# K and V chunks as one transfer over 128 partitions instead of two over alternate partitions

## The chip, the cores and the metric

The kernel runs on one core of a Trainium2 chip. The metric is the device time of one execution in microseconds (us), lower is better. The kernel before took 215.94 us (median of 3 runs, 215.93 to 216.82). A run counts as slow when it is over 1.5% above the fastest run of the same kernel; all comparisons below use fast runs, unless a sentence says otherwise.

Some terms. HBM is the large memory where the inputs lie, SBUF the memory on the chip with 128 rows, called partitions. PE (TensorE) does the matrix products, VectorE (DVE) and ScalarE (ACT) the rest, and the sync queue (SP) issues transfers. A transfer is one issued load; the 16 DMA engines carry it out in packets, and each engine ends its part with a 4-byte semaphore packet that reports it done. A transfer has landed when all 16 have reported. The cadence is the time from the landing of one chunk to the landing of the next.

## The reference, cut to what matters

One decoding step: an attention block over a long cache, beside a small mixer and MLP block, added together.

```python
# x [4, 1, 576]; k_cache, v_cache [B=4, Hkv=16, Sk=8192, Dh=128], bf16; 32 query heads
W = min(4096, max(256, Sk // 4))                   # 2048: only the last 2048 tokens count
k = jnp.repeat(k_cache[:, :, Sk - W:, :], 2, axis=1)
v = jnp.repeat(v_cache[:, :, Sk - W:, :], 2, axis=1)
p = softmax(einsum("bhqd,bhkd->bhqk", q, k) * Dh ** -0.5)
o = einsum("bhqk,bhkd->bhqd", p, v) ... @ wo
# + B block: layernorm, w1 [576, 576], w2, w3 [576, 4608], w4 [4608, 576]
```

The windows of K and V have 4 x 16 x 2048 x 128 bf16 elements each, 33.6 MB. Both together are 67.1 MB of the 88.5 MB that the kernel has to read. Each byte is loaded once.

## The kernel before

K and V come in 16 chunks each. A chunk is one batch and four heads (2 MB); it fills one of the four slots of a ring in SBUF. Partition 4i + g of a slot holds 64 tokens in a row of head g: 16384 bytes that are contiguous in HBM and in SBUF. All loads but the small x are issued from one queue, the sync queue. A slot is refilled when PE has transposed (K) or multiplied (V) what was in it.

```python
NPOS = 4                                    # slots of the ring
ring_t = sb("ring", [128, NPOS * UE], BF16) # UE = 64 tokens x 128 = 8192 elements
...
def kv_pairs(cache, c):                     # the two halves of a chunk
    b, gq = CH[c]
    dst = lambda a: ring_t[a:128:2, (c % NPOS) * UE:(c % NPOS + 1) * UE]
    src = cache[b, NU * gq:NU * gq + NU, Sk - W:Sk, :].rearrange("g (i t) d -> i g (t d)", t=NT)
    return [(dst(a), src[:, a:NU:2, :]) for a in range(2)]
for c in range(NC):
    add_dma(kv_pairs(A_k_cache, c), ("k", c % NPOS), [t_done(c - NPOS)] if c >= NPOS else [], c)
for c in range(NC):
    add_dma(kv_pairs(A_v_cache, c), ("v", c % NPOS), [f"PV{c - NPOS}" if c >= NPOS else t_done(c + NC - NPOS)], KS + c)
...
# PE: before the first transpose of a K chunk, and before the products of a V chunk
w = [take(("k", c % NPOS), 32)] if k == 0 else []     # 16 for each of the two halves
...
# every such wait is emitted in one helper (line 584 of the kernel)
engine.wait_ge(S[w[1]], w[2]).then_inc(S[w[1]], -w[2])
```

A half has 64 partitions, every second one. PE waits for both halves of a chunk, so the halves are never used one by one.

## Time and profile before

| | before |
|---|---|
| time, median of 3 | 215.94 us |
| span in the profile | 214.1 us |
| moved by DMA | 88.66 MB, 7459 packets |
| K and V issues | 64 of 1024 KB |
| 16384-byte data packets | 4096 for K and V, median 613 ns |

The last row is from the packet records of the trace. The next lines are from the page of the kernel before: the span; the busy share of the 16 DMA engines in 40 slices (9 is nine tenths or more) and the GB/s of each slice; the packets; the sync queue's own row (packets, MB, share of the engines' time); the lines of the chain that ended last; and the K and V issues with the KB of each and the median us from issue to landing.

```profile
span 214.1 us, 5906 instructions
...
DMA  7999999999999999999999999999999999999992
GB/s 282 404 385 445 441 407 438 419 427 416 435 429 429 422 435 429 424 426 435 429 426 426 429 429 425 419 432 429 429 422 429 435 429 419 430 436 426 428 409 104
DMA packets 7459, 88.66 MB, mean 414 GB/s; under 512 B 1292, under 2 KB 1688, under 8 KB 2456
...
q1 hardware_dynamic: 7432, 88.50, 97.7%
...
DMA w<-in_B_w_dram 15%; SPq L177 1%; PE ps L421 1%; PE ps L438 1%; DVE out_sb L560 0%
...
ring<-in_A_k_cache_dram SPq DMA_DIRECT2D x32, 1024.0 KB, 13.0
ring<-in_A_v_cache_dram SPq DMA_DIRECT2D x32, 1024.0 KB, 15.1
```

The DMA engines are at nine tenths or more in every slice but the first and the last. A K half lands 13.0 us after its issue although it takes 2.4 us to move: the rest is waiting behind other transfers in the queue.

The stretch table of the kernel before gives, for each stretch, busy us of each engine with the number of instructions, then the granted clock, the DMA share (packet time over the time of 16 engines; it can pass 1 because the records of neighbouring packets overlap by a few ns) and GB/s:

```profile
core 0: us, PE busy (x) PEld busy (x) DVE busy (x) ACT busy (x) POOL busy (x), PEclk, DMA share, GB/s
...
34.00:100.00 66.00, 64.26 (x1060) 51.74 (x1052) 42.06 (x66) 39.84 (x43) 3.81 (x13) 1.00 1.01 427
100.00:130.00 30.00, 21.69 (x389) 16.53 (x388) 17.42 (x29) 16.34 (x23) 0.00 (x0) 0.82 1.01 428
130.00:180.00 50.00, 19.63 (x674) 18.97 (x674) 4.69 (x14) 0.00 (x0) 0.00 (x0) 0.50 1.01 427
```

From 34 to 180 us the DMA share is 1.01, whatever PE does: PE is busy 64.26 of 66 us in the K stage and 19.63 of 50 us in the V stage, and the rate is 427 or 428 GB/s in both. The Trainium skill ("DMA: Bandwidth & Descriptors", Specifications) gives 435 GB/s as the ceiling on the SBUF side; the trace agrees to 2%.

The sync queue's own waits (us in total, times, longest) show that the queue that issues the transfers has nothing to do most of the time:

```profile
SPq L177 <- PE ps L340: 84.8, 16, 27.9
SPq L177 <- PE ps L421: 46.1, 12, 11.0
SPq L177 <- DVE out_sb L560: 31.8, 1, 31.8
```

And one line from PE's waits:

```profile
engine line waited for: us in total, times, longest us
PE ps L421 <- PEq L584: 37.7, 13, 3.2
```

The wait is put down to PE's sequencer at line 584. That is the helper line of the kernel that takes a semaphore.

The end of the chain in order of time (start, us, what):

```profile
179.19 31.22 DMA w<-in_B_w_dram
...
210.46 1.39 PE ps L438 x18
211.85 0.44 DVE out_sb L560
```

A w4 load that was issued at 179.2 us lands at 210.4 us, and PE, VectorE and the store follow.

### The profile page before, as it was taken

To read this page: it belongs to the slowest core of one execution; us is meant where nothing else is said; L and a number is where in the kernel's file an instruction comes from. 1 tells how busy PE (TensorE), PEld (TensorE's weight loads), DVE (VectorE), ACT (ScalarE), POOL (GpSimd) and SP (SyncE) were. 2 spreads that over 40 slices of the span, in tenths; PEclk is the share of its full clock that TensorE was granted. 3 is DMA by queue.
4 is the path that set the end of the run, shared out by engine and by line. 5 is a ranking of instruction groups with operands and counts; after the bars stand their busy time and mean duration, and the time that the engine had idled before them with its cause. 6 is when DMAs were issued, how large, how long until landed. Compare 5 with 4: busy or idle time off the path is not lost. (4 is left out here: it accounts for less than half of the span.)

```text
span 214.1 us, 5906 instructions
## 1 busy us (share of the span) xinstructions
PE 145.6 (68%) x2642; PEld 108.9 (51%) x2646; DVE 76.5 (36%) x150; ACT 61.0 (29%) x75; POOL 10.9 (5%) x37
## 2 busy tenths in 40 slices
PE   0157787999999999999996178033444333336995
PEld 0023312888878887888774068033434333334542
DVE  5305400577676676666664830100010011001000
ACT  2001402466655665666666620000000000000000
POOL 8301000000001000000000000000000000000000
PEclk9999699999999999999999655555555555555799
DMA  7999999999999999999999999999999999999992
GB/s 282 404 385 445 441 407 438 419 427 416 435 429 429 422 435 429 424 426 435 429 426 426 429 429 425 419 432 429 429 422 429 435 429 419 430 436 426 428 409 104
DMA packets 7459, 88.66 MB, mean 414 GB/s; under 512 B 1292, under 2 KB 1688, under 8 KB 2456
## 3 DMA queue, kind: packets, MB, share of 16 engines
q1 hardware_dynamic: 7432, 88.50, 97.7%
q8 instruction: 8, 0.13, 0.2%
q14 instruction: 3, 0.02, 0.0%
q10 hardware_dynamic: 16, 0.01, 0.0%
HBM read 88.49 MB, written 0.00 MB: 413 GB/s over the span
## 5 line engine op out<-in xcount | busy, mean ns | idle before, releaser
L340 PE MATMUL ps<-perm_bf,ring 128*128 128x128 bf16 x1024 | 61.7, 220 | 0.6
L340 PEld LDWEIGHTS ps<-perm_bf,ring 128*128 128x128 bf16 x1024 | 57.5, 98 | 8.9 <-issue 8.6
L347 DVE COPY kt<-ps 128x1024 bf16<-128x1024 bf16 x80 | 52.3, 687 | 24.8 <-PE ps L340 24.3
L421 PE MATMUL ps<-PTpad,ring 128*128 128x8 bf16 x1024 | 29.7, 168 | 41.2 <-PEq L584 37.7
L346 ACT ACTIVATE kt<-ps 128x1024 bf16<-128x1024 bf16 x48 | 48.5, 1023 | 29.1 <-PE ps L340 28.3
L421 PEld LDWEIGHTS ps<-PTpad,ring 128*128 128x128 bf16 x1024 | 28.7, 104 | 42.3 <-issue 42.2
L561 ACT ACTIVATE out_sb<-ps 4x288 bf16<-4x288 f32 x1 | 0.4, 401 | 87.2 <-PE ps L438 87.2
L354 PE MATMUL ps<-kt,Qs 128*32 128x512 bf16 x272 | 17.8, 382 | 1.4 <-PEq L584 1.4
L410 DVE TENSOR_TENSOR PTpad<-PT,mU_bf 128x512 bf16<-128x512 bf16 x16 | 6.4, 420 | 29.7 <-PE ps L421 29.7
L433 DVE TENSOR_TENSOR OTn<-ps,rinvB 128x32 bf16<-128x32 f32 x4 | 0.8, 191 | 34.2 <-PE ps L421 34.2
L523 PE MATMUL ps<-w,x1nT 128*32 128x384 bf16 (+2 forms) x65 | 11.3, 766 | 0.8 <-DMA w<-in_B_w_dram 0.5
L354 PEld LDWEIGHTS ps<-kt,Qs 128*32 128x32 bf16 x272 | 5.8, 96 | 6.8 <-issue 1.5
L375 POOL COPY Qs<-Qpad 128x128 bf16<-128x128 bf16 x16 | 4.6, 293 | 87.0 <-PE ps L354 75.0
L301 PE MATMUL ps<-kt,xnT 128*32 128x512 bf16 x32 | 3.6, 631 | 4.3 <-DMA kt<-in_A_wq_dram 4.3
L523 PEld LDWEIGHTS ps<-w,x1nT 128*32 128x32 bf16 x65 | 3.3, 113 | 6.3 <-issue 3.9
L438 PE MATMUL ps<-w,ORT 128*4 128x288 bf16 x64 | 5.8, 357 | 0.4 <-DVE ORT L460 0.4
L278 PE MATMUL ps<-ident_bf,xn_bf 4*128 4x4 bf16 x8 | 0.6, 170 | 8.0 <-DVE ragsrc L271 8.0
L560 DVE CAST out_sb<-ps 4x288 bf16<-4x288 f32 x1 | 0.4, 446 | 14.5 <-PE ps L438 14.5
L438 PE MATMUL ps<-w,h2T_sb 128*4 128x288 bf16 x72 | 5.0, 286 | 0.4 <-DMA w<-in_B_w_dram 0.4
L392 PE MATMUL ps<-kt,permT_bf 128*128 128x512 bf16 x3 | 1.8, 608 | 4.9 <-DVE kt L391 4.8
L544 DVE COPY h2T_sb<-ps 128x16 bf16<-128x16 bf16 x1 | 0.2, 166 | 13.6 <-PE ps L538 13.6
L438 PEld LDWEIGHTS ps<-w,ORT 128*4 128x4 bf16 x64 | 3.3, 106 | 3.1 <-DVE ORT L460 1.0
(99 smaller groups left out, 61.6 us busy)
## 6 DMA issues: line engine op xcount, KB each, us to landing
ring<-in_A_k_cache_dram SPq DMA_DIRECT2D x32, 1024.0 KB, 13.0
ring<-in_A_v_cache_dram SPq DMA_DIRECT2D x32, 1024.0 KB, 15.1
w<-in_B_w_dram SPq DMA_DIRECT2D x2, 2304.0 KB, 22.9
w<-in_A_wo_dram SPq DMA_DIRECT2D x2, 2304.0 KB, 20.3
kt<-in_A_wq_dram SPq DMA_DIRECT2D x1, 4096.0 KB, 12.2
w<-in_B_w_dram SPq DMA_DIRECT2D x1, 2592.0 KB, 27.4
w<-in_B_w_dram SPq DMA_DIRECT2D x3, 576.0 KB, 14.5
w<-in_B_w_dram SPq DMA_DIRECT2D x1, 1296.0 KB, 30.0
```

Source lines behind the costliest of these rows:

```text
L301: ins = e.matmul(Qps[k][32 * g:32 * g + 32, :], lhsT=x_, rhs=w, start=(r == 0), stop=(r == 4), tile_position=(0, 32 * g), skip_group_check ...
L340: ins = e.transpose(tb[n % 4][:, t, :], slot_t(c)[:, 8 * k + t, :], perm_bf[:])
L346: return "act", lambda e: e.activation(out=ktbuf[:, n % 16], in_=tb[n % 4], func=ACTF.Copy)
L347: return "dve", lambda e: e.tensor_copy(out=ktbuf[:, n % 16], in_=tb[n % 4])
L354: ins = e.matmul(Sps[32 * u:32 * u + 32, q, :].rearrange("p (t i) -> p t i", t=16), lhsT=Qs[:, c % NPOS, 32 * u:32 * u + 32], rhs=ktgrp[:, ...
L375: P(lambda e, c=c, cc=cc: e.tensor_copy(out=Qs[:, c % NPOS, :], in_=Qpad_t[:, 128 * cc:128 * cc + 128]), waits=["qT", "qs_zero"] + ([f"SC{ ...
L392: add("pe", lambda e, q=q: e.matmul(ps[:, 4 + q % 3, :], lhsT=permT_bf[:], rhs=PTx[:, q, :], start=True, stop=True), waits=[f"PTx{q}", "pe ...
L410: return lambda e: e.tensor_tensor(out=PTpad[:, c % 2], in0=PTv[:, :, cc, :].unsqueeze(2).to_broadcast([128, NT, NU, 2]), in1=mU_bf[:].uns ...
L421: ins = e.matmul(o_, lhsT=slot_t(c)[:, t, :], rhs=PTpad[:, c % 2, t].rearrange("p u e -> p (u e)"), start=(t == 0), stop=(t == NT - 1))
L433: add("dve", lambda e, hv=hv: e.tensor_tensor(out=hv(OTn), in0=OTps.rearrange("p (b h) -> p b h", b=B), in1=hv(rinvB), op=ALU.mult), waits ...
L438: return e.matmul(ACC[h], lhsT=lhsT, rhs=rhs, start=start, stop=stop, tile_position=(0, 32 * h), skip_group_check=True)
L523: ins = e.matmul(H2ps[k][32 * g:32 * g + 32, 128 * off:128 * (off + cnt)].rearrange("p (c x) -> p c x", c=cnt), lhsT=x_, rhs=w.rearrange(" ...
```

## The change

The intent: half as many transfers for K and V, each twice as large, all partitions at once; fewer issues and fewer completions for the same bytes.

```diff
         def kv_pairs(cache, c):
             b, gq = CH[c]
-            dst = lambda a: ring_t[a:128:2, (c % NPOS) * UE:(c % NPOS + 1) * UE]
-            src = cache[b, NU * gq:NU * gq + NU, Sk - W:Sk, :].rearrange("g (i t) d -> i g (t d)", t=NT)
-            return [(dst(a), src[:, a:NU:2, :]) for a in range(2)]
+            return [(ring_t[:, (c % NPOS) * UE:(c % NPOS + 1) * UE],
+                     cache[b, NU * gq:NU * gq + NU, Sk - W:Sk, :].rearrange("g (i t) d -> i g (t d)", t=NT))]
...
-                w = [take(("k", c % NPOS), 32)] if k == 0 else []
+                w = [take(("k", c % NPOS), 16)] if k == 0 else []
...
-            ... take(("v", c % NPOS), 32) ...
+            ... take(("v", c % NPOS), 16) ...
```

More of the change, by code (lines that the diff above doesn't have):

```diff
@@ L428, in bass_parallel_sum__sliding_block_cached__mixer_s_mlp__decode_kernel @@
             add("dve", dve_pad(c), waits=w, inc=[(tok("pad"), 1)], key=KV + 2 * max(c - 1, 0) + 0.2)
-            add("pe", pe_PV(c), waits=[take("pad"), take(("v", c % NPOS), 32)] + ([take("otn")] if b == 0 else []), sig=f"PV{c}",
+            add("pe", pe_PV(c), waits=[take("pad"), take(("v", c % NPOS), 16)] + ([take("otn")] if b == 0 else []), sig=f"PV{c}",
                 key=KV + 2 * c, loop=("V", gq))
```

## The prediction

> **What bounds the kernel now.** The DMA engines, all the time. The page of the kernel before moves 88.66 MB in a span of 214.1 us, DMA at nine tenths in all slices but the first and last. The stretch table has a DMA share of 1.01 at 427 to 428 GB/s from 34 to 180 us. The chain of waits ends in a w4 load that was issued at 179.2 us and landed at 210.4, plus 18 matmuls, one copy and the store. No wait of PE for a K or V load is in the list of waits. The Trainium skill ("DMA: Bandwidth & Descriptors", Specifications) gives a ceiling of 435 GB/s at the SBUF side; this trace is within 2% of it in these stretches.
>
> **What the change does.** It removes 32 of 64 transfers of 1024 KB: 32 issues on the sync queue (median 600 ns for K, 572 ns for V) and, per DMA engine, 32 semaphore packets of 4 bytes (9 ns each in the trace's packet records). It adds nothing. The data packets stay 4096 of 16384 bytes, median 613 ns; only their order changes (four heads in turn instead of two and two). The compute engines' order is the same. PE waited for both halves before, so the grain of compute, the ring and the issue waits stay. The same skill page (Rules for kernel authors) says that two transfers to disjoint partition sets serialize on the same 16 engines and one transfer should be used. It doesn't say how large the gain is in a full queue.
>
> **How much is on the critical path.** Sync queue: none. A K chunk takes 4.89 us to move (from the landings), issuing its halves took about 1.2 us, and a half lands a median 13.0 us (K) or 15.1 us (V) after issue, so its fixed costs hide behind queued transfers. Semaphore packets: at most 32 x 9 ns = 0.29 us per engine. Comparing cadences suggests less: the halves land every 2.446 us, that is 611.6 ns per packet with its quarter of a semaphore; the second wo load (eight packets of 18432 bytes per engine, one semaphore) took 5.50 us and the first w4 load (eight of 20736) 6.18 us. From these three I estimate 0.0368 ns per byte, some 10 ns per packet, and about zero for a transfer. So the gain is between 0 and 0.3 us of 215.9.
>
> **Prediction.** 215.7 us, 8 in 10 between 215.0 and 216.7 (the three runs before spread from 215.93 to 216.82). Chances: faster by over 2% 0.01, within 2% 0.95, slower by over 2% 0.04.
>
> **What would show it.** K and V as 32 transfers of 2048 KB with the DMA share still 1.01 and 426 to 430 GB/s in the same stretches; a K chunk landing every 4.88 to 4.90 us; 16384-byte packets still at 613 ns; about 512 fewer small packets; the chain still ending in the same w4 load at about 210 us.
>
> **What would make it wrong.** Another order of reads (each engine now steps through four heads 2 MB apart) that slows packets above 613 ns: 3% would cost 5 us. Two engines meeting at one port. A longer stall at the first K issue (5.6 us now, from 5.3) that runs the queue dry. A different placing of the instruction fetches, which already leave some engines 1.9 us behind others at the end (landing records of the last w4 load): about 1 us either way.

## The result, and the profile after

| | before | after |
|---|---|---|
| median us (6 runs each) | 216.02 (215.91 to 217.14) | 216.04 (215.88 to 216.50) |
| ratio of the fast runs | | 0.9991, 95% interval 0.9966 to 1.0015 |
| K and V issues | 64 of 1024 KB | 32 of 2048 KB |

Ratios here and below are the mean time of one kernel's fast runs over that of the kernel before in the same rounds, so they are not quite the ratio of the medians in the text. The time is the same. The lines of the page of the changed kernel that answer to those above:

```profile
span 214.7 us, 5874 instructions
...
DMA  7999999999999999999999999999999999999992
GB/s 276 409 381 443 436 413 433 437 424 411 412 424 430 433 433 424 427 429 433 421 430 424 427 436 419 427 427 430 424 427 424 430 430 427 427 432 432 417 413 78
DMA packets 6946, 88.65 MB, mean 413 GB/s; under 512 B 780, under 2 KB 1176, under 8 KB 1944
...
q1 hardware_dynamic: 6920, 88.50, 97.4%
...
DMA w<-in_B_w_dram 15%; SPq L177 1%; PE ps L420 1%; PE ps L437 0%; DVE out_sb L559 0%
...
ring<-in_A_k_cache_dram SPq DMA_DIRECT2D x16, 2048.0 KB, 11.5
ring<-in_A_v_cache_dram SPq DMA_DIRECT2D x16, 2048.0 KB, 16.6
```

The same bytes, 513 packets fewer (the counts under 512 B fell from 1292 to 780, which is 32 semaphore packets on each of 16 engines), and the same share and rate in the slices. A K chunk lands 11.5 us after its issue (a half 13.0), a V chunk 16.6 us (a half 15.1).

The stretch table of the changed kernel, same columns:

```profile
34.00:100.00 66.00, 64.64 (x1038) 52.03 (x1029) 41.10 (x64) 38.31 (x42) 3.52 (x12) 0.97 1.01 427
100.00:130.00 30.00, 22.61 (x402) 17.58 (x396) 18.41 (x31) 17.06 (x24) 0.29 (x1) 0.85 1.01 428
130.00:180.00 50.00, 20.16 (x695) 19.45 (x692) 4.70 (x14) 0.00 (x0) 0.00 (x0) 0.50 1.01 427
```

The DMA share and the rate did not move: 1.01 at 427, 428 and 427 GB/s.

The sync queue's waits after the change:

```profile
SPq L177 <- PE ps L339: 100.9, 16, 32.7
SPq L177 <- PE ps L420: 52.7, 12, 11.7
SPq L177 <- DVE out_sb L559: 33.1, 1, 33.1
```

The three totals were 84.8 + 46.1 + 31.8 = 162.7 us and are now 100.9 + 52.7 + 33.1 = 186.7 us, 24.0 us more. Issuing K and V took 41.8 us before and takes 23.2 us now; the 18.6 us that the queue saved went into waits: it is done issuing sooner and then waits longer for PE to empty a slot.

The end of the chain after the change:

```profile
178.91 32.92 DMA w<-in_B_w_dram
...
211.88 0.58 PE ps L437 x6
212.46 0.43 DVE out_sb L559
```

It still ends in a w4 load, but in the next of the five, 1.4 us later; that load landed at 211.11 us before, so it is 0.7 us later here. (In the second trace of the changed kernel, below, the chain ends in the same load as before, at 210.8 us.) This profiled run was the slowest of the six (216.5 us), with a span 0.6 us longer. The landing records show where that comes from. The 16 engines finish the last w4 load between 209.58 and 212.06 us here, and between 209.54 and 211.47 us before: the first engine is done at the same time, and the last one lags by 2.47 us instead of 1.93 us.

The landing records also give the cadence: when the last engine's share of K chunk 0 and of K chunk 15 landed, and the difference divided by 15. It is worked out from the traces for all the kernels that leave the queue open:

```
kernel              chunk 0    chunk 15   us per chunk   data packet, median / mean ns
before              36.35      109.74     4.893          16384 B: 613 / 614.9
after               36.31      109.88     4.904          16384 B: 613 / 615.9
after_again         36.31      109.79     4.898          16384 B: 614 / 615.6
four_by_head        36.39      109.81     4.894          16384 B: 611 / 614.3
two_by_column       36.23      110.99     4.984           8192 B: 313 / 314.0
eight_by_column     36.61      112.14     5.035           8192 B: 309 / 318.0
contiguous_halves   42.41      185.28     9.525          16384 B: 1206 / 1189.3
```

A chunk in one transfer takes as long as a chunk in two, to within 0.011 us.

### The profile page after: what moved, and what is told of

Read it like the earlier page. It is cut to its first block, busy times and chain, and to the rows that moved or that the text cites. A ratio compares the mean times of both kernels' runs of the same rounds, so it can differ in the third digit from the quotient of the medians.

```text
span 214.7 us, 5874 instructions
## 1 busy us (share of the span) xinstructions
PE 147.2 (69%) x2642; PEld 111.2 (52%) x2646; DVE 76.2 (35%) x150; ACT 60.2 (28%) x75; POOL 10.9 (5%) x37
## 2 busy tenths in 40 slices
DMA packets 6946, 88.65 MB, mean 413 GB/s; under 512 B 780, under 2 KB 1176, under 8 KB 1944
## 5 line engine op out<-in xcount | busy, mean ns | idle before, releaser
L339 PEld LDWEIGHTS ps<-perm_bf,ring 128*128 128x128 bf16 x1024 | 58.8, 99 | 7.1 <-issue 6.8
L345 ACT ACTIVATE kt<-ps 128x1024 bf16<-128x1024 bf16 x48 | 47.7, 1023 | 29.3 <-PE ps L339 29.3
L522 PE MATMUL ps<-w,x1nT 128*32 128x384 bf16 (+1 forms) x65 | 11.1, 766 | 0.4 <-DVE x1nT L497 0.4
L437 PE MATMUL ps<-w,ORT 128*4 128x288 bf16 x64 | 5.0, 324 | 0.4 <-DVE ORT L459 0.4
L437 PEld LDWEIGHTS ps<-w,h2T_sb 128*4 128x4 bf16 x72 | 2.8, 84 | 4.0 <-DMA w<-in_B_w_dram 3.0
## 6 DMA issues: line engine op xcount, KB each, us to landing
ring<-in_A_k_cache_dram SPq DMA_DIRECT2D x16, 2048.0 KB, 11.5
ring<-in_A_v_cache_dram SPq DMA_DIRECT2D x16, 2048.0 KB, 16.6
```

The costliest lines, as they stand in the source:

```text
L339: ins = e.transpose(tb[n % 4][:, t, :], slot_t(c)[:, 8 * k + t, :], perm_bf[:])
L345: return "act", lambda e: e.activation(out=ktbuf[:, n % 16], in_=tb[n % 4], func=ACTF.Copy)
L437: return e.matmul(ACC[h], lhsT=lhsT, rhs=rhs, start=start, stop=stop, tile_position=(0, 32 * h), skip_group_check=True)
L522: ins = e.matmul(H2ps[k][32 * g:32 * g + 32, 128 * off:128 * (off + cnt)].rearrange("p (c x) -> p c x", c=cnt), lhsT=x_, rhs=w.rearrange(" ...
```

## The experiments

Theory A: the DMA engines are the bound, and a transfer has next to no cost of its own while others are queued behind it. Rival B: a transfer does cost something, and the changed order of reads lost as much as the merging gained. Rival C: PE, busy 97% of the K stage, is the real bound, so nothing done to DMA can show. Where no base is named, the edits are to the kernel before.

### The changed kernel again, and four transfers per chunk

The first is the changed kernel as it is, with five rounds.

> The changed kernel once more, for a narrower interval. Theory A (the DMA engines are the bound, and a transfer in a full queue costs next to nothing by itself): ratio to the kernel before 0.998 to 1.001, that is 0 to 0.3 us. Rival B (each transfer removed gains its fixed cost, but the new order of reads loses as much): the same ratio, so this run alone does not tell them apart; B needs 16384-byte packets slower than 613 ns, which the trace of the first run does not show.

Measured: 216.10 us against 216.14 us, ratio 0.9989 (0.9968 to 1.0010). The same again.

The second has one transfer per head, 512 KB each, so 64 transfers more than before:

```diff
-            dst = lambda a: ring_t[a:128:2, ...]
+            dst = lambda a: ring_t[a:128:4, ...]
-            return [(dst(a), src[:, a:NU:2, :]) for a in range(2)]
+            return [(dst(a), src[:, a:a + 1, :]) for a in range(NU)]
-                w = [take(("k", c % NPOS), 32)] ...      # and the same for V
+                w = [take(("k", c % NPOS), 64)] ...
```

> Each chunk as four transfers of 512 KB, one head each: 64 transfers more than the kernel before, same packets of 16384 bytes, another order of reads. Theory A: between 0 and +0.6 us (64 times at most one 9 ns semaphore packet), chunk still every 4.89 us, packets at 613 ns. Rival B (a transfer has a real cost in the queue, which the changed kernel's read order hid): clearly slower, for 0.1 us per transfer +6 us.

Measured: 216.06 us, ratio 0.9990 (0.9969 to 1.0010). Lines of its page:

```profile
DMA packets 8483, 88.66 MB, mean 413 GB/s; under 512 B 2316, under 2 KB 2712, under 8 KB 3480
...
ring<-in_A_k_cache_dram SPq DMA_DIRECT2D x64, 512.0 KB, 8.6
ring<-in_A_v_cache_dram SPq DMA_DIRECT2D x64, 512.0 KB, 13.3
```

One, two and four transfers per chunk, with three different orders of reads, take 216.1, 216.1 and 216.1 us; the cadence is 4.898, 4.893 and 4.894 us. For rival B to hold at any size that matters, the order of reads would have to cancel the cost at all three counts, and the packets would have to be slower by as much. Their means are 615.6, 614.9 and 614.3 ns: 1.3 ns between the ends, times 256 packets per engine, is 0.3 us. A trade of that size between packets and transfers can't be excluded, since the times don't resolve it. Theory A stands. The interval leaves room for the predicted gain of 0 to 0.3 us (0.14%), but not for 0.1 us per transfer.

### Smaller packets, same number of transfers

Two transfers over all 128 partitions, each with half the columns:

```diff
-            dst = lambda a: ring_t[a:128:2, (c % NPOS) * UE:(c % NPOS + 1) * UE]
+            HU = UE // 2
+            dst = lambda a: ring_t[:, (c % NPOS) * UE + a * HU:(c % NPOS) * UE + (a + 1) * HU]
-            return [(dst(a), src[:, a:NU:2, :]) for a in range(2)]
+            return [(dst(a), src[:, :, a * HU:(a + 1) * HU]) for a in range(2)]
```

> Two transfers of 1 MB per chunk as before, but over all 128 partitions and half the columns each, so 8192-byte packets, twice as many. From the estimate of 10 ns per packet (256 more per DMA engine) theory A expects +2.4 us, ratio about 1.011, the chunk every 5.04 us. If only the number of transfers or of partitions mattered, it would be +0.0.

Measured: 218.30 us, ratio 1.0093 (1.0073 to 1.0112), 2.16 us more than the median before. Lines of its page and of its stretch table:

```profile
DMA packets 11555, 88.66 MB, mean 410 GB/s; under 512 B 1292, under 2 KB 1688, under 8 KB 2456
...
q1 hardware_dynamic: 11528, 88.50, 98.2%
```

```profile
34.00:100.00 66.00, 63.38 (x1040) 50.71 (x1035) 41.38 (x64) 39.17 (x43) 3.81 (x13) 1.00 1.01 421
```

So the split that keeps the number of transfers costs 2.16 us, and the split that doubles it at the same packet size (four_by_head) costs nothing. The packets count, not the transfers. The 4096 additional packets are 256 per engine: 2.16 us / 256 = 8.4 ns each in the time; the cadence of K says (4.984 - 4.893) us / 8 = 11.4 ns. That cadence is a mean which two long gaps (5.05 and 5.08 us) raise; by the medians of the gaps, 4.974 and 4.893 us, it is 10.1 ns. The estimate was 10. Whether the cost is the packet's own or comes from the shorter run that is read from HBM, this run does not separate. The cadence of 5.04 us in the expectation was an error of arithmetic: 4.893 us plus 8 x 10 ns is 4.97 us.

### Eight transfers per chunk

Head by head and half the columns, 256 KB each, with the packets of the experiment above:

```diff
+            HU = UE // 2
+            dst = lambda g, a: ring_t[g:128:4, (c % NPOS) * UE + a * HU:(c % NPOS) * UE + (a + 1) * HU]
+            return [(dst(g, a), src[:, g:g + 1, a * HU:(a + 1) * HU]) for a in range(2) for g in range(NU)]
```

> Eight transfers of 256 KB per chunk (one head, half the columns), 8192-byte packets as in the two-by-column kernel, 192 transfers more than it. Theory A: within 0 to +1.7 us of the two-by-column kernel as long as the sync queue can issue eight in 4.9 us (8 times 0.53 to 0.60 us is 4.3 to 4.8, just enough). Rival B: far slower; if issue becomes the limit the DMA share drops below 1 and the sync queue shows no waits.

Measured: 220.87 us median, but scattered from 218.54 to 222.45 us. Two of the six runs count as slow, the profiled one too; they look like the upper end of the scatter, for a fast run had as low a clock (0.788 against 0.790 and 0.791). The four fast ones give a ratio of 1.0162 (1.0120 to 1.0205), 1.5 us more than the two-by-column kernel (1.0162 - 1.0093 of 216 us). The chain of its profiled run and a line of its stretch table:

```profile
SPq L177 14%; DMA w<-in_B_w_dram 10%; PE ps L422 1%; PE ps L439 1%; DVE out_sb L561 0%
```

```profile
34.00:100.00 66.00, 64.62 (x1035) 52.04 (x1032) 41.08 (x64) 38.21 (x42) 3.52 (x12) 0.97 1.01 409
```

Now the sync queue is 14% of the chain: issuing eight transfers at a median of 594 ns takes 4.75 us of a cadence of about 5 us, and its waits fall to 42.0 us in all (154.9 in the two-by-column kernel). So the issue comes close to being the limit. That it is one, this run does not show: the DMA share stays at 1.01 in the line above (at 409 GB/s in place of 421), and the expectation named a share below 1 and no waits as the signs. Because of the scatter it gives no clean cost per transfer either. It agrees with the range expected (0 to 1.7 us), no more.

### Where the fixed cost is: one transfer in flight

The queue waits for every K and V transfer to land before it issues the next. It is done once with the changed kernel (32 transfers of 2 MB) and once with the kernel before (64 of 1 MB). As the waiting takes the semaphore, the queue itself tells PE afterwards:

```diff
+        def add_alone(pairs, skey, waits, key):
+            def emit(e):
+                for o_, i_ in pairs:
+                    e.dma_start(o_, i_).then_inc(S["lone"], 16)
+                    e.wait_ge(S["lone"], 16).then_inc(S["lone"], -16)
+                e.sem_inc(S[skey], 16)        # 32 in the kernel with two halves
+            add("sp", emit, waits, None, key)
-            add_dma(kv_pairs(A_k_cache, c), ...)   # and the same for V
+            add_alone(kv_pairs(A_k_cache, c), ...)
```

> The changed kernel, but the sync queue waits for each K and V transfer to land before it issues the next: one transfer of 2 MB in flight. This exposes a transfer's fixed cost. [...] Theory A expects 32 transfers with about 2 us each exposed: +55 to +75 us over 216, each 6.5 to 7.2 us from issue to landing.

> The kernel before, with the same wait after each of its 64 transfers of 1 MB. Theory A expects twice the fixed cost of the one-transfer form: a difference between the two of 32 times about 2 us, +50 to +75 us, so about 330 to 350 us in all. Rival (merging never matters, whatever the queue holds): the two forms equal.

Measured: 305.82 us in the first, 376.84 us in the second (the kernel before on the same chip: 216.59 us). The DMA row and the K and V issues, of the first and then of the second:

```profile
DMA  8999567665766777766676668576666766678994
...
ring<-in_A_k_cache_dram SPq DMA_DIRECT2D x16, 2048.0 KB, 7.3
ring<-in_A_v_cache_dram SPq DMA_DIRECT2D x16, 2048.0 KB, 7.4
```

```profile
DMA  8996555555555555545655547555555555555795
...
ring<-in_A_k_cache_dram SPq DMA_DIRECT2D x32, 1024.0 KB, 4.8
ring<-in_A_v_cache_dram SPq DMA_DIRECT2D x32, 1024.0 KB, 4.8
```

The DMA engines now stand idle between transfers. The kernel with half the transfers is 71.0 us faster, 71.0 / 32 = 2.22 us for each transfer less. Against the open queue the exposed cost is (305.82 - 216.59) / 32 = 2.79 us per transfer of 2 MB and (376.84 - 216.59) / 64 = 2.50 us per transfer of 1 MB. The 2 us of both expectations is the fixed cost that the Trainium skill ("DMA: Bandwidth & Descriptors", Anatomy of one DMA) gives for transfers on the gpsimd path (about 2.0 us). These transfers go by the sync queue, and they show somewhat more; the issue (a median of 534 to 535 ns in both traces) is a part of it. So both totals were expected too low: the first at +55 to +75 us, measured +89, with 7.3 us to landing in place of 6.5 to 7.2; the second at 330 to 350 us, measured 376.84. The difference between the two, 71.0 us, is inside the +50 to +75 expected, and the rival (no difference) falls. So the cost that the change removes is real, and it is large where it is exposed. In the kernel as it is, it is not exposed.

### How full the queue has to be

The kernel before with at most two transfers of 1 MB in flight: before each issue the queue waits for the transfer before the last one.

```diff
+                for n, (o_, i_) in enumerate(pairs):
+                    if len(flight) == 2:      # 3 in the third kernel
+                        land(e)               # wait for the oldest; tell PE if its chunk is whole
+                    k = count[0] % 2
+                    count[0] += 1
+                    e.dma_start(o_, i_).then_inc(S[("pair", k)], 16)
+                    flight.append((k, skey if n == 1 else None))   # 2 MB transfers: skey always
```

> The kernel before, with at most two transfers of 1 MB in flight: the sync queue waits for the transfer before the last one to land before each issue. Theory A: a fixed cost of about 2 us fits under the other transfer's 2.45 us, so nearly all of it vanishes: 216 to 225 us, DMA share 0.95 or more in the middle.

Measured: 229.64 us, ratio 1.0609 (1.0558 to 1.0659), more than the 216 to 225 us expected; the DMA share from 34 to 100 us was 0.93, below the 0.95 expected:

```profile
34.00:100.00 66.00, 59.88 (x934) 48.09 (x932) 37.48 (x58) 35.83 (x39) 3.26 (x11) 0.95 0.93 371
```

Two runs were made to see what two in flight lack: a third transfer of 1 MB, and two of 2 MB with the changed kernel.

> At most three transfers of 1 MB in flight, where two gave 229.6 us (13 us more than an open queue, more than expected). Theory D: what two in flight lost is not only the fixed cost but the engines' lag behind each other (1.5 to 2 us after an instruction fetch), which one transfer of slack cannot cover; a third transfer (2.45 us more) covers both: 216 to 219 us. Rival E (the waits themselves cost the sync queue time at every transfer): still 225 us or more.

> The changed kernel with at most two transfers of 2 MB in flight. Theory D: the slack is one whole transfer of 4.9 us, which covers the fixed cost of about 2.4 us and a lag of 2 us: 216 to 219 us, so that with a shallow queue the larger transfer does gain, some 11 us against two transfers of 1 MB in flight. Rival E, a cost for every wait: half of the 13 us, 222 us.

Measured: 219.78 us for three of 1 MB (218.94 and 220.62; ratio 1.0177, 1.0084 to 1.0269), a little over the 216 to 219 us expected. A line of the stretch table of its profiled run, a fast one:

```profile
150.00:190.00 40.00, 14.30 (x499) 13.93 (x500) 2.99 (x9) 0.00 (x0) 0.00 (x0) 0.50 0.98 401
```

For two of 2 MB, 221.94 us in a fast run and 226.89 us in a slow one. That was repeated with five rounds:

> The same kernel as the one with two transfers of 2 MB in flight, because one of its two runs was in the slow state (226.9 us) and the other fast (221.9 us). If theory D's slack of a whole transfer were enough, its fast runs would be at 216 to 219 us; the one fast run says about 222 us. The trace should show where the loss sits: in idle DMA engines (DMA share below 1) or in longer packets (mean of the 16384-byte packets above 615 ns at a DMA share of 1).

Measured: 218.79, 219.31 and 220.31 us in the three fast runs, 222.37 to 223.02 us in the three slow ones; ratio 1.0155 (1.0131 to 1.0179). A line of the stretch table of its profiled run, which is a slow one:

```profile
150.00:190.00 40.00, 13.50 (x469) 13.12 (x470) 2.99 (x9) 0.00 (x0) 0.00 (x0) 0.50 1.00 400
```

With two transfers in flight the merged form is faster after all: 1.0155 against 1.0609 of the kernel before, about 10 us. That figure leaves out half of its runs as slow, but the order does not hang on this: the slowest of its eight runs (226.89 us) is below the faster one with two of 1 MB (229.19 us). But neither three of 1 MB nor two of 2 MB gets all the way back to 216 us, as theory D had it. Rival E, a cost for every wait, is out, since three in flight waits as often as two and loses 3.8 us in place of 13. Where the last 3 us sit is only partly told. In the slow profiled run the DMA share is 1.00 at 400 GB/s, and over the run the 16384-byte packets took a mean of 637 ns in place of 615: the engines are not idle, some packets are longer. The fast run with three of 1 MB shows much the same, a share of 0.98 at 401 GB/s and a mean of 626 ns. It is not all packets: their median is 611 ns in both runs (613 before), but 215 and 133 of the 4096 took over 700 ns, against 8 in the kernel before. Why these few take longer in a short queue, no run here shows.

### Which halves

The kernel before with halves that are 64 partitions in a row:

```diff
-            dst = lambda a: ring_t[a:128:2, ...]
+            dst = lambda a: ring_t[64 * a:64 * a + 64, ...]
-            return [(dst(a), src[:, a:NU:2, :]) for a in range(2)]
+            return [(dst(a), src[NI // 2 * a:NI // 2 * (a + 1)]) for a in range(2)]
```

> Two transfers of 1 MB per chunk, 16384-byte packets as before, but on partitions 0 to 63 and 64 to 127 instead of alternate ones. The Trainium skill (SBUF - State Buffer, Door 1: The DMA port swizzle) says that 64 partitions in a row reach only 8 of the 16 ports. If the 16 DMA engines then meet in pairs at the ports, a packet takes about twice 613 ns and K and V (67 MB) take 150 us longer: about 365 us. If a full queue lets the two halves overlap, or the ports do not matter: 216 us.

Measured: 364.24 us, ratio 1.6866, within 1 us of the 365 expected. A line of its stretch table:

```profile
60.00:170.00 110.00, 69.36 (x924) 54.63 (x928) 38.70 (x58) 34.82 (x34) 3.26 (x11) 0.85 1.01 220
```

The share is 1.01 as ever, so a share of 1 does not mean that the engines move all they can: the packets take 1206 ns in place of 613, and the rate is 220 GB/s. The Trainium skill ("SBUF - State Buffer", Door 1: The DMA port swizzle) says that 64 partitions in a row reach 8 of the 16 ports; the trace agrees with half the rate. The halves on alternate partitions of the kernel before, and the merged transfer, do not meet this: their packets take 613 ns.

### Is it the bytes?

The changed kernel with only 32 KB loaded for the last V chunk. Its output is wrong, which doesn't matter for the time.

```diff
+            pairs = kv_pairs(A_v_cache, c)
+            if c == NC - 1:
+                pairs = [(o_[:, 0:Dh], i_[:, :, 0:Dh]) for o_, i_ in pairs]
-            add_dma(kv_pairs(A_v_cache, c), ("v", c % NPOS), ...)
+            add_dma(pairs, ("v", c % NPOS), ...)
```

> The changed kernel with 32 KB instead of 2 MB loaded for the last V chunk; the result is wrong on purpose. Compute is unchanged. Theory A (bytes through the DMA engines set the time): 4.8 us less, 211.2 us, ratio about 0.978. Rival C (PE, busy 64.3 of the 66 us from 34 to 100, sets the time): no change.

Measured: 212.09 us against 216.59 us, ratio 0.9795 (0.9755 to 0.9836). Lines of its page:

```profile
DMA packets 6946, 86.59 MB, mean 412 GB/s; under 512 B 908, under 2 KB 1304, under 8 KB 2072
...
PE ps L440 5%; PE ps L446 2%; PE ps L423 2%; DVE out_sb L562 0%; DVE ORT L462 0%; DVE OTn L435 0%; PE ps L460 0%
```

With 2.06 MB less (86.59 against 88.65) and all the compute, the time fell by 4.5 us by the medians, 4.4 by the ratio. Rival C falls. The 0.3 us or so that are missing to 4.8 have a place: the chain no longer ends in a load. It is PE for 9% of the span, from the last V products to the end, so PE was only a few microseconds behind the DMA at the end and has taken over there.

## Why the prediction was right

- **What bounds the kernel.** Right: bytes through the DMA engines. Taking 2 MB away took 4.5 us; the share stayed at 1.01 and 427 to 428 GB/s in every stretch named.
- **What the change removes.** Right in count: 32 issues and 512 small packets fewer. The issue time turned into 24 us more waiting on the sync queue, which costs nothing.
- **The size.** Predicted 0 to 0.3 us of gain; measured ratios 0.9991 and 0.9989, each with an interval of about 0.2% to both sides. Zero and 0.3 us are both inside. The runs can't tell one from the other, so the size within this range is not confirmed. What says more than the ratio is the row of one, two and four transfers per chunk, with 4.898, 4.893 and 4.894 us per chunk in one trace each.
- **The estimate by size of packet.** About 10 ns per packet and about zero per transfer came from three cadences in the trace of before. The column experiment measured 8.4 ns (time) to 11.4 ns (mean cadence) per packet.
- **What would show it.** The packets stayed at 613 ns. The cadence was 4.904 us in the profiled run, just outside the 4.88 to 4.90 named, and 4.898 us in the second. The chain ended in the next w4 load, at 211.8 instead of about 210 us, as the slowest engine lagged more in that run; in the second trace it ended in the load named, at 210.8 us.
- **One reading was loose.** "No wait of PE for a K or V load is in the list of waits" is true of the list's words only. The 37.7 us put down to PE's sequencer at the helper line are PE waiting for V chunks. Read rightly, they support the argument rather than harm it.
- **The dangers named.** The order of reads did no harm in three orders. Two engines meeting at one port would fit the contiguous halves (364 us, packets of 1206 ns), though no trace names the port; it is no danger of this change. The first K issue stalled 5.8 us instead of 5.6 and the queue did not run dry.

## What to carry to other kernels

Before merging transfers, look at the DMA share and at the time from issue to landing. Here the share was 1.01 and a half landed 13.0 us after its issue, with 2.4 us to move; its fixed cost was already hidden, and merging gave nothing. With one transfer in flight each transfer less gave back 2.2 us, with two some 0.3 us (about 10 us for 32). In a full queue it was the size of the contiguous run (the packet) and the set of partitions that mattered: a packet cost about 10 ns on top of its bytes, and halves on 64 partitions in a row doubled the median time of a packet (613 to 1206 ns) with the DMA share still at 1.01. So a share of 1 alone doesn't tell that nothing is left to gain.

## What the Trainium skill lacked or had wrong

- "DMA: Bandwidth & Descriptors", Rules for kernel authors: the row on disjoint partition halves advises one transfer of 128 partitions. It lacks that halves on alternate partitions in a full queue cost nothing (ratio of the merged form 0.999), while with halves of 64 partitions in a row the kernel takes 1.69 times as long (364.2 us; see "Which halves" above).
- The same page, fixed cost of about 2.0 us per transfer: it is given for the gpsimd path. On the sync queue, with one transfer in flight, waited for by the queue, these runs show 2.2 to 2.8 us. The page lacks how many have to be in flight before it vanishes: 376.8 us with one of 1 MB, 229.6 with two, 219.8 with three, 216 with the queue open.
- The same page gives costs per packet for small descriptors, in cycles and as the floor of a 4 KB transfer. None has it for large ones: 8 to 11 ns per packet between 8192 and 16384 bytes.
- "SBUF - State Buffer", Summary: rules for kernel authors, advises about 358 GB/s for loads from HBM. This program on one core held 427 to 428 GB/s for 146 us; the page "HBM Reference" has the higher number for a core that streams alone.
- "Runtime: NRT & Kernel Launch", Instruction fetch mechanics, has the blocks of 16 KiB. It lacks what they may cost the data: in the trace of before, eight such packets took 1.01 to 1.10 us each, some data packets right after them took as long in place of 613 ns, and the engines ended 1.9 us apart. That the fetches cause the whole of that lag is argued, not shown.
